# A sliding-window attention and token/channel MLP on one core: fixed buffers and program order on every engine, full 128x128 weight tiles with paired tails, q and k transposed by DMA

## The chip, the cores and the metric

One core of a Trainium2 chip. The metric is the device time of one execution in microseconds (us), as the median of several runs. The kernel before took 393.35 us (three runs, 390.92 to 396.79).

The engines are called by the profile's names: PE (TensorE, matmuls), PEld (its weight loads, which overlap PE), DVE (VectorE), ACT (ScalarE), POOL (GpSimd) and SP (SyncE). POOL issues the loads that cast float32 to bf16, SP the outputs. In the kernels' code PE writes its results into PSUM tiles, which the text also calls banks; those of the new kernel have names that begin with `ps`. `L373` is line 373 of the kernel in question, so line numbers differ from kernel to kernel.

## The reference

Eight batches of 576 tokens, eight heads of 64. Causal attention over a window of 128 keys with a linear bias per head, then an MLP that mixes over tokens and one that mixes over channels.

```
scores = q @ k.T / 8 + slope[h] * -(i - j)         # kept where 0 <= i - j < 128
attn   = softmax(scores) @ v                        # B, H, 576, 64
x      = attn as (B, 576, 512)
h      = relu(x.T @ w_tok1) @ w_tok2                # 576 -> 256 -> 576, over tokens
u      = x + h.T
out    = u + relu(u @ w_ch1) @ w_ch2                # 512 -> 1536 -> 512, over channels
```

576 is four and a half times 128. The half block, 64 tokens, is the tail that this case is largely about.

## The kernel before

A framework schedules it: pools hand out buffers, and the scheduler orders each engine. The MLP of batch b is mixed with the attention of batch b+1. q and k come in token order and are transposed on PE, five blocks per head pair, the last with 64 rows:

```python
for c in range(NCH):                      # 128, 128, 128, 128, 64 tokens
    nc.tensor.transpose(tps[:, s0 : s0 + nn],
                        cbt[tname][:nn, c, hp * 2 * D : (hp + 1) * 2 * D], ident[:nn, :nn])
```

Attention goes by query block and four heads; PV follows the masks of the same four heads at once:

```python
for h in hs:
    nc.scalar.activation(out=pe[:, :, 0:nq], in_=sp[:, i : i + 3 : 2, 0:nq],
                         func=ACT.Exp, bias=biascol[:, h : h + 1], scale=scale)   # one head
    nc.vector.tensor_tensor(out=pb[:, :, 0:nq], in0=pe[:, :, 0:nq], in1=mk[:, :, 0:nq], op=ALU.mult)
# ...
for mi, (o_ap, l_ap, r_ap) in enumerate(mms):        # 65 columns each: 64 of v and a 1
    nc.tensor.matmul(o_ap, lhsT=l_ap, rhs=r_ap, start=(mi == 0), stop=(mi == len(mms) - 1))
```

The second channel matmul makes five passes per batch over the 12 weight blocks, the fifth for 64 tokens only:

```python
for c in range(NCH):
    nq = csz[c]                           # 64 in the last pass
    for ht_i in range(NHT):
        nc.tensor.matmul(o2[:nq, :], lhsT=r2[ht_i][:, c * P : c * P + nq], rhs=WC2[:, ht_i, :], ...)
```

The softmax here doesn't subtract the row's maximum and nothing guards it: scores larger than these inputs give would overflow.

Of the kernel before, what the change touches and what calls it, by code (L numbers as in the profile page):

```python
# [10 lines left out]
ALU = mybir.AluOpType  # L12

DMA_TRANSPOSE_QK = False
DMA_TRANSPOSE_U = False
# [3 lines left out]
def kernel(  # L19
# [11 lines left out]
    nc = tc.nc  # L31
    P = nc.NUM_PARTITIONS

# [5 lines left out]

    assert D == 64 and H % 4 == 0  # L40
    NCH = (S + P - 1) // P
    csz = [min(P, S - c * P) for c in range(NCH)]
    NHP = H // 2
    NQD = H // 4

    slopes = [2.0 ** (-8.0 * (h + 1) / H) for h in range(H)]

    bf16 = mybir.dt.bfloat16
    f32 = mybir.dt.float32

    NDH = DTOK // P
    NCB = DM // P
    NHT = DCH // P
    assert DTOK % P == 0 and DM % P == 0 and DCH % P == 0 and S % 2 == 0
    SH = S // 2

    const = ctx.enter_context(tc.tile_pool(name="const", bufs=1))
    qkpool = ctx.enter_context(tc.tile_pool(name="qk", bufs=2))
    stage = ctx.enter_context(tc.tile_pool(name="stage", bufs=3))
    cbpool = ctx.enter_context(tc.tile_pool(name="cbp", bufs=2))  # L60
    vpool = ctx.enter_context(tc.tile_pool(name="vpl", bufs=2))
    ppool = ctx.enter_context(tc.tile_pool(name="pp", bufs=8))
    xpool = ctx.enter_context(tc.tile_pool(name="xp", bufs=2))
    rpool = ctx.enter_context(tc.tile_pool(name="rp", bufs=2))
    upool = ctx.enter_context(tc.tile_pool(name="up", bufs=2))
    opool = ctx.enter_context(tc.tile_pool(name="op", bufs=3))
    ps_sc = ctx.enter_context(tc.tile_pool(name="ps_sc", bufs=3, space=bass.MemoryType.PSUM))
    ps_ov = ctx.enter_context(tc.tile_pool(name="ps_ov", bufs=2, space=bass.MemoryType.PSUM))
    ps_ma = ctx.enter_context(tc.tile_pool(name="ps_ma", bufs=3, space=bass.MemoryType.PSUM))

    ident = const.tile([P, P], bf16, name="ident")
    make_identity(nc, ident)
    pidx = const.tile([P, 1], f32, name="pidx")
    nc.gpsimd.iota(
        pidx, pattern=[[0, 1]], base=0, channel_multiplier=1,
        allow_small_or_imprecise_dtypes=True,
    )
    biascol = const.tile([P, H], f32, name="biascol")
    for h in range(H):
        nc.gpsimd.tensor_scalar(  # L80
            out=biascol[:, h : h + 1], in0=pidx[:, 0:1],
            scalar1=float(slopes[h]), scalar2=None, op0=ALU.mult,
        )
    patA = const.tile([P, P], bf16, name="patA")
    patB = const.tile([P, P], bf16, name="patB")
    nc.gpsimd.memset(patA[:, :], 1.0)
    nc.gpsimd.affine_select(
        out=patA[:, :], in_=patA[:, :],
        compare_op=ALU.is_gt, fill=0.0, base=0,
        pattern=[[-1, P]], channel_multiplier=1,  # L90
    )
    nc.gpsimd.memset(patB[:, :], 1.0)
    nc.gpsimd.affine_select(
        out=patB[:, :], in_=patB[:, :],
        compare_op=ALU.is_ge, fill=0.0, base=0,
        pattern=[[1, P]], channel_multiplier=-1,
    )

    def _alloc_batch_tiles():
        cbq = cbpool.tile([P, NCH, H * D], bf16, name="cbq", tag="cbq")  # L100
        cbk = cbpool.tile([P, NCH, H * D], bf16, name="cbk", tag="cbk")
        vp = vpool.tile([P, NCH, H, D + 1], bf16, name="vp", tag="vp")
        nc.vector.memset(vp[:, :, :, D : D + 1], 1.0)
        return {"q": cbq, "k": cbk}, vp

    def _dma_qk_chunk(b, cbt, tname, c):
        tens = q if tname == "q" else k
        nn = csz[c]
        s0 = c * P
        nc.gpsimd.dma_start(  # L110
            out=cbt[tname][:nn, c, :].rearrange("p (h d) -> p h d", h=H),
            in_=tens[b, :, s0 : s0 + nn, :].rearrange("h s d -> s h d"),
        )

    def _dma_v_chunk(b, vp, c):
        nn = csz[c]
        s0 = c * P
        nc.gpsimd.dma_start(  # L118
            out=vp[:nn, c, :, 0:D],
            in_=v[b, :, s0 : s0 + nn, :].rearrange("h s d -> s h d"),  # L120
        )

    def attention_dma(b):
        cbt, vp = _alloc_batch_tiles()
        for c in range(NCH):
            _dma_qk_chunk(b, cbt, "q", c)
            _dma_qk_chunk(b, cbt, "k", c)
        for c in range(NCH):
            _dma_v_chunk(b, vp, c)
        return cbt, vp  # L130

    cbt0, vp0 = _alloc_batch_tiles()
    head_chunks = min(2, NCH)
    for c in range(head_chunks):
        _dma_qk_chunk(0, cbt0, "q", c)
        _dma_qk_chunk(0, cbt0, "k", c)
    _dma_v_chunk(0, vp0, 0)
    for c in range(head_chunks, NCH):
        _dma_qk_chunk(0, cbt0, "q", c)
        _dma_qk_chunk(0, cbt0, "k", c)  # L140
    for c in range(1, NCH):
        _dma_v_chunk(0, vp0, c)
    sts_first = (cbt0, vp0)

    qTz = [[const.tile([P, 2, S], bf16, name=f"qTz{hp}_{par}") for hp in range(NHP)]
           for par in range(2)]
    for hp in range(NHP):
        nc.vector.memset(qTz[0][hp][D:P, 0, :], 0.0)
        nc.vector.memset(qTz[0][hp][0:D, 1, :], 0.0)

    masks = const.tile([P, H, 2 * P], bf16, name="masks")
    for h in range(H):
        chA = math.exp(-float(P) * slopes[h])
        nc.vector.tensor_scalar(
            out=masks[:, h, 0:P], in0=patA[:, :],
            scalar1=float(chA), scalar2=None, op0=ALU.mult,
        )
        nc.vector.tensor_copy(out=masks[:, h, P : 2 * P], in_=patB[:, :])

    def attention_steps(b, dma_res, xb):  # L160
        cbt, vp = dma_res
        yield
        qT = []
        kT = []
        for hp in range(NHP):
            for tname in ("q", "k"):
                tps = ps_sc.tile([P, S], bf16, name="tTps", tag="sc")
                for c in range(NCH):
                    nn = csz[c]
                    s0 = c * P  # L170
                    nc.tensor.transpose(  # L171
                        tps[:, s0 : s0 + nn],
                        cbt[tname][:nn, c, hp * 2 * D : (hp + 1) * 2 * D],
                        ident[:nn, :nn],
                    )
                if tname == "k":
                    tt = qkpool.tile([P, S], bf16, name=f"kT{hp}", tag=f"kT{hp}")
                    nc.vector.tensor_copy(out=tt[:, :], in_=tps[:, :])
                    kT.append(tt)
                else:  # L180
                    tt = qTz[b % 2][hp]
                    nc.vector.tensor_copy(out=tt[0:D, 0, :], in_=tps[0:D, :])
                    nc.vector.tensor_copy(out=tt[D:P, 1, :], in_=tps[D:P, :])
                    qT.append(tt)
                yield
        for qb in range(NCH):
            nq = csz[qb]
            q0 = qb * P
            have_a = qb > 0
            nkb = nq  # L190
            for qd in range(NQD):
                hs = [4 * qd + j for j in range(4)]
                hps = [2 * qd, 2 * qd + 1]
                sps = {}
                for hp in hps:
                    sp = ps_sc.tile([P, 4, P], f32, name="sp", tag="sc")
                    sps[hp] = sp
                for half in (0, 1):
                    if half == 0 and not have_a:
                        continue  # L200
                    for hp in hps:
                        spf = sps[hp][:, :, :].rearrange("p b x -> p (b x)")
                        if half == 0:
                            nc.tensor.matmul(  # L204
                                spf[:, 0 : 2 * nq],
                                lhsT=kT[hp][:, q0 - P : q0],
                                rhs=qT[hp][:, :, q0 : q0 + nq],
                                start=True, stop=True,
                            )
                        else:  # L210
                            nc.tensor.matmul(  # L211
                                spf[:nkb, 2 * P : 2 * P + 2 * nq],
                                lhsT=kT[hp][:, q0 : q0 + nkb],
                                rhs=qT[hp][:, :, q0 : q0 + nq],
                                start=True, stop=True,
                            )
# [186 lines left out]
    for b in range(B):  # L403
# [3 lines left out]
        if pending_mlp is not None:  # L407
            gens.append(pending_mlp)
# [56 lines left out]
```

## Time and profile before

| | before |
|---|---|
| median of 3 runs | 393.35 us |
| span of the profiled run | 396.0 us |
| PE busy | 370.6 us (94%) |
| DVE, ACT, POOL busy | 241.0, 195.7, 109.2 us |
| distance between batches | 44.9 us |

Part 1 of the page of the kernel before gives busy time, share of the span and number of instructions of each engine:

```profile
PE 370.6 (94%) x2752; PEld 206.7 (52%) x2752; DVE 241.0 (61%) x792; ACT 195.7 (49%) x593; POOL 109.2 (28%) x147
```

The view by time windows of the kernel before has, per stretch: its length, then busy us and number of instructions of PE, PEld, DVE, ACT and POOL, then the clock granted to PE, the DMA share and GB/s:

```profile
36.00:47.00 11.00, 10.27 (x55) 4.92 (x56) 4.26 (x23) 2.04 (x10) 7.41 (x9) 0.55 0.91 150
60.00:70.00 10.00, 9.93 (x95) 6.74 (x93) 5.34 (x22) 9.61 (x31) 8.06 (x11) 1.00 3.33 126
200.00:210.00 10.00, 9.98 (x94) 5.86 (x93) 7.33 (x29) 8.70 (x27) 3.08 (x4) 1.00 1.20 77
```

After the start PE is hardly ever free, and no other engine is near it. But a busy PE is not a PE at its peak: matmul intervals overlap (190 ns long and 30 ns apart in the new kernel below), so their union hides gaps between starts. The Trainium skill warns of this ("Perfetto Trace Analysis", section "Identifying the Most-Contended Engine": matmul occupancy is no good measure of the distance to the roofline).

The chain of waits of the kernel before (start, duration, what) has the first token-mix matmuls of successive batches, and at its end the last channel matmuls:

```profile
89.61 1.29 PE t_1350 L320 x5
134.50 1.29 PE t_2083 L320 x5
179.40 1.29 PE t_2816 L320 x5
...
359.00 1.29 PE t_5728 L320 x5
...
386.77 2.59 PE o_6001 L388 x12
```

Batches are 44.9 us apart. The last line is the clean rate: twelve matmuls of 512 columns in 2.59 us, 216 ns each.

The timeline of PE in the kernel before (start, duration, line, what, shapes, count) shows how small matmuls stand among large ones:

```profile
138.72 0.20 PE L171 MATMUL tTps<-ident,cbq 64*128 64x64 bf16 x1
138.85 0.34 PE L171 MATMUL tTps<-ident,cbk 128*128 128x128 bf16 x3
...
153.34 0.19 PE L273 MATMUL ot<-vp,pb 128*128 128x65 bf16 x1
153.37 0.27 PE L211 MATMUL sp<-qTz_1_141,kT_2269 128*128 128x256 bf16 x1
153.57 0.20 PE L273 MATMUL ot<-vp,pb 128*128 128x65 bf16 x1
```

Start to start is what counts. After the 64-row transpose at 138.72 the next matmul starts 130 ns later, though it streams half a block. PV matmuls (L273) come one at a time; by the view of waits their weight loads waited 115 times for the mask product, never longer than 0.5 us, 30.3 us in all.

### The profile page before, as it was taken

How to read it: one execution, taken by the hardware profiler on the slowest of the kernel's cores; microseconds unless marked ns; L12 is line 12 of the kernel's file. 1: busy time of each engine (PE TensorE's matmuls, PEld its weight loads, DVE VectorE, ACT ScalarE, POOL GpSimd, SP SyncE). 2: the span in 40 equal slices, each digit the busy share in tenths (PEclk: the TensorE clock that was granted, in tenths of full speed). 3: DMA queues.
4: the chain of work that ended last, by engine and by line, in shares of the span. 5: the costliest groups of instructions: out<-in, count | busy, mean ns of one | idle time of the engine just before them, and what ended most of it. 6: DMA issues, size and time to landing. Idle time of an engine off the chain costs nothing.

```text
span 396.0 us, 7388 instructions
## 1 busy us (share of the span) xinstructions
PE 370.6 (94%) x2752; PEld 206.7 (52%) x2752; DVE 241.0 (61%) x792; ACT 195.7 (49%) x593; POOL 109.2 (28%) x147
## 2 busy tenths in 40 slices
PE   0387999999999999999999999999999999999996
PEld 0143466544754466544764466544764466543752
DVE  7277474766577485766577485776577575765112
ACT  0077229641694238641694328741594327842620
POOL 9996427504440408004350307004000000000000
PEclk9998599999999999999999999999999999999999
DMA  7999999929392379629291379719001200011012
GB/s 48 138 138 100 181 189 129 141 85 73 26 96 79 59 45 86 64 79 74 19 104 53 82 48 81 67 62 91 2 1 55 66 2 0 28 56 40 2 38 82
DMA packets 120804, 27.81 MB, mean 70 GB/s; under 512 B 113280, under 2 KB 115648, under 8 KB 120768
## 3 DMA queue, kind: packets, MB, share of 16 engines
q0 software_dynamic: 115520, 17.90, 72.0%
q1 hardware_dynamic: 5248, 9.44, 6.6%
q8 instruction: 21, 0.34, 0.4%
q14 instruction: 15, 0.12, 0.1%
HBM read 35.78 MB, written 9.44 MB: 114 GB/s over the span
## 4 chain that ended last, share of the span: by engine, by line
PE 87%; POOL 7%; DMA 2%; DVE 2%; ACT 1%; issue 1%; POOLq 0%; ACTq 0%
PE ct L373 23%; PE ot L273 9%; PE tTps L171 6%; PE ht L335 5%; PE sp L211 4%; PE ut L359 3%; PE sp L204 3%; POOL cbq L110 2%; POOL vp L118 2%; POOL cbk L110 2%; DMA W_168<-in_moe_w_tok_dram 2%; DVE ub L341 1%; PE o_5654 L388 1%; PE o_4940 L388 1%; PE o_4207 L388 1%
## 5 line engine op out<-in xcount | busy, mean ns | idle before, releaser
L379 ACT ACTIVATE r2t<-ct 128x288 bf16<-128x288 f32 x192 | 77.4, 454 | 71.6 <-PE ct L373 65.4
L373 PE MATMUL ct<-utt,WC_170 128*128 128x288 bf16 x768 | 110.7, 286 | 0.0
L229 ACT ACTIVATE pe<-sp,biascol 128x256 bf16<-128x256 f32 x192 | 79.1, 587 | 22.7 <-PE sp L211 22.7
L373 PEld LDWEIGHTS <-WC_170 128*128 128x128 bf16 x768 | 69.1, 98 | 16.1
L273 PEld LDWEIGHTS <-pb 128*128 128x128 bf16 (+2 forms) x576 | 41.3, 101 | 67.8 <-DVE pb L233 30.3
L273 PE MATMUL ot<-vp,pb 128*128 128x65 bf16 (+2 forms) x576 | 73.0, 203 | 2.7 <-DVE pb L242 1.2
L118 POOL DMA_DIRECT2D vp<-in_v_dram x40 | 33.8, 870 | 100.0 <-PE o_3532 L388 21.3
L233 DVE TENSOR_TENSOR pb<-pe,masks 128x256 bf16<-128x256 bf16 x192 | 51.8, 287 | 6.4
L388 PEld LDWEIGHTS <-r2t 128*128 128x128 bf16 (+1 forms) x480 | 41.5, 100 | 24.3 <-issue 0.4
L110 POOL DMA_DIRECT2D cbq<-in_q_dram x40 | 35.4, 887 | 52.1 <-PE tTps L171 32.7
L278 DVE RECIPROCAL rt<-ot 128x4 f32<-128x4 f32 (+1 forms) x80 | 14.5, 181 | 41.4 <-PE ot L273 41.1
L341 DVE TENSOR_TENSOR ub<-ht,xb 128x512 bf16<-128x512 f32 (+1 forms) x40 | 24.8, 681 | 22.0 <-PE ht L335 22.0
L110 POOL DMA_DIRECT2D cbk<-in_k_dram x40 | 35.4, 888 | 7.6 <-DMA WC_171<-in_moe_w_ch_dram 6.7
L247 ACT ACTIVATE pe<-sp,biascol 64x64 bf16<-64x64 f32 x64 | 20.0, 313 | 34.0 <-PE sp L211 34.0
L279 DVE TENSOR_TENSOR xb<-ot,rt 128x256 bf16<-128x256 f32 (+1 forms) x80 | 33.9, 423 | 2.0
L171 PE MATMUL tTps<-ident,cbq 128*128 128x128 bf16 (+1 forms) x160 | 20.9, 232 | 11.4 <-DMA cbq<-in_q_dram 11.4
L171 PEld LDWEIGHTS <-cbq 128*128 128x128 bf16 (+1 forms) x160 | 12.6, 101 | 23.8 <-DMA cbq<-in_q_dram 12.2
L171 PE MATMUL tTps<-ident,cbk 128*128 128x128 bf16 (+1 forms) x160 | 20.3, 230 | 4.2 <-DMA cbk<-in_k_dram 3.5
L335 PE MATMUL ht<-r1t,W_169 128*128 128x512 bf16 (+1 forms) x80 | 23.8, 398 | 0.3
L242 DVE TENSOR_TENSOR pb<-pe,masks 128x128 bf16<-128x128 bf16 x64 | 13.2, 223 | 15.9 <-ACT pe L238 14.9
L252 ACT ACTIVATE pe<-sp,biascol 128x64 bf16<-128x64 f32 x64 | 20.0, 313 | 0.0
L171 PEld LDWEIGHTS <-cbk 128*128 128x128 bf16 (+1 forms) x160 | 12.5, 102 | 13.2 <-DMA cbk<-in_k_dram 4.6
(332 smaller groups left out, 454.1 us busy)
## 6 DMA issues: line engine op xcount, KB each, us to landing
out_dram<-obt SPq DMA_DIRECT2D x32, 256.0 KB, 2.0
cbq<-in_q_dram POOLq DMA_DIRECT2D x32, 128.0 KB, 5.1
cbk<-in_k_dram POOLq DMA_DIRECT2D x32, 128.0 KB, 5.3
vp<-in_v_dram POOLq DMA_DIRECT2D x32, 128.0 KB, 5.6
WC_170<-in_moe_w_ch_dram POOLq DMA_DIRECT2D x1, 1536.0 KB, 13.3
WC_171<-in_moe_w_ch_dram POOLq DMA_DIRECT2D x1, 1536.0 KB, 20.2
out_dram<-obt SPq DMA_DIRECT2D x8, 128.0 KB, 3.0
cbq<-in_q_dram POOLq DMA_DIRECT2D x8, 64.0 KB, 5.1
```

Of the source, the lines that this page charges most:

```text
L110: nc.gpsimd.dma_start(out=cbt[tname][:nn, c, :].rearrange("p (h d) -> p h d", h=H), in_=tens[b, :, s0 : s0 + nn, :].rearrange("h s d -> s ...
L118: nc.gpsimd.dma_start(out=vp[:nn, c, :, 0:D], in_=v[b, :, s0 : s0 + nn, :].rearrange("h s d -> s h d"),)
L171: nc.tensor.transpose(tps[:, s0 : s0 + nn], cbt[tname][:nn, c, hp * 2 * D : (hp + 1) * 2 * D], ident[:nn, :nn],)
L229: nc.scalar.activation(out=pe[:, :, 0:nq], in_=sp[:, i : i + 3 : 2, 0:nq], func=ACT.Exp, bias=biascol[:, h : h + 1], scale=scale,)
L233: nc.vector.tensor_tensor(out=pb[:, :, 0:nq], in0=pe[:, :, 0:nq], in1=mk[:, :, 0:nq], op=ALU.mult,)
L273: nc.tensor.matmul(o_ap, lhsT=l_ap, rhs=r_ap, start=(mi == 0), stop=(mi == len(mms) - 1),)
L279: nc.vector.tensor_tensor(out=xb[:nq, qb, hs[0] * D : (hs[-1] + 1) * D].rearrange("p (h d) -> p h d", h=4), in0=ot[:nq, :, 0:D], in1=rt[:n ...
L335: nc.tensor.matmul(ht[:nq, :], lhsT=W2[:, j, c * P : c * P + nq], rhs=r1[j][:, :], start=(j == 0), stop=(j == NDH - 1),)
L341: nc.vector.tensor_tensor(out=ub[:nq, c, :], in0=ht[:nq, :], in1=xb[:nq, c, :], op=ALU.add)
L373: nc.tensor.matmul(ct[:, :], lhsT=WC1[:, cb, ht_i * P : (ht_i + 1) * P], rhs=utb[cb][:, x * SH : (x + 1) * SH], start=(cb == 0), stop=(cb ...
L379: nc.scalar.activation(out=r2t[:, x * SH : (x + 1) * SH], in_=ct[:, :], func=ACT.Relu)
L388: nc.tensor.matmul(o2[:nq, :], lhsT=r2[ht_i][:, c * P : c * P + nq], rhs=WC2[:, ht_i, :], start=(ht_i == 0), stop=(ht_i == NHT - 1),)
```

## The change

The intent: PE is the bound, so take work off it, make every weight tile 128x128, and lay out by hand what comes when. The diff replaces nearly the whole kernel; its core:

```diff
+    ctx.enter_context(tc.manual_schedule())          # program order on all engines
+    psS = [PS(f"psS{i}", [P, 512]) for i in range(2)]; psO = PS("psO", [P, 2, 512])
+    psM = [PS(f"psM{i}", [P, 512]) for i in range(3)]; psT = PS("psT", [P, 512])
 # --- q and k: on PE only for batches 0 and 1
-    nc.tensor.transpose(tps[:, s0 : s0 + nn], cbt[tname][:nn, c, ...], ident[:nn, :nn])
+    def dma_transpose(b):
+        nc.sync.dma_start_transpose(out=kT[i][:, 0:NC]..., in_=kn...)
+        nc.sync.dma_start_transpose(out=kT[i][:, NC, :, 0:ST], in_=knt[:, :])
+        nc.sync.dma_start_transpose(out=qT[i]..., in_=qn...)      # q padded with zeros, 2 x the bytes
+        nc.sync.dma_start_transpose(out=qTt[i]..., in_=qnt...)
 # --- attention by key block: the queries of a key block and of the next one, two heads
+    nc.tensor.matmul(s[:, :], lhsT=kT[i][:, kb, hp, :], rhs=qT[i][:, kb:kb + 2, hp, :, :], ...)
+    nc.scalar.activation(out=e[:, 0:nn], in_=s[:, 0:nn], func=ACT.Exp, scale=scale)   # 512 wide
+    # mask multiply (with the bias in the mask) issued one piece later, PV four pieces later
 # --- tails: two heads side by side in attention, two batches in the second channel matmul
+    nc.tensor.matmul(t[:, :], lhsT=r2t[pi2][:, ht, :, :], rhs=WC2[:, ht, :], ...)     # 2 x 64 tokens
 # --- first channel matmul: 512 columns plus 64
-    rhs=utb[cb][:, x * SH : (x + 1) * SH]                       # 2 x 288
+    rhs=utb[b % 2][:, cb, :]                                     # 512, tail apart
 # --- four of twelve relus on DVE
 # [...] loads, evictions and the order of pieces are cut
+    for it in spread(main, carry):  run(it)     # first channel matmul with 8 pieces of attention b+1
+    for it in spread(seq, fill):    run(it)     # second one and token mix of b+1, with attention b+2
```

## The prediction

> **What bounds the kernel now.** TensorE. In the table of ten-microsecond windows PE is busy 9.9 of every 10 us from 40 to 360 us at clock 1.00. The chain of waits shows the first token-mix matmul (L320) at 89.6, 134.5, 179.4, ... 359.0: 44.9 us per batch, with a head of about 45 us and a tail of 37 us (last MLP alone). I count 88,392 streamed columns per batch. Twelve 512-column matmuls at the end take 2.59 us (216 ns each), so the ideal is 36.8 us; about 8 us per batch are lost around small matmuls. Start-to-start times in the steady timeline: q,k transposes 3.8 us per batch (84 ns per 128x128 one, 135 per 64-row one), 64-row contractions and 64-wide weight tiles 60 to 100 ns dearer, 65-column PV 40 to 110 ns.
>
> **What the change does to PE, per batch.**
> - PE transposes of q,k: removed for batches 2 to 7 (-3.8 us).
> - Tails paired: every weight tile is 128x128; one tail pass of the second channel matmul for two batches (10 passes -> 9). The first becomes 48 of 512 columns plus 48 of 64.
> - Sum from 216 ns per 512 columns and an estimated 37 ns for a tight 64- or 65-column matmul (five of 65 columns end to end in 0.33 us): scores 3.5, PV 2.6, token mix 4.4, u transposes 1.1, channel one 12.3, channel two 11.9 = 36 us. With 1 to 2 us of buffer waits (three rotated PSUM banks) 37 to 38 us per batch.
>
> ACT falls: one 512-column exp per head pair and key block (a 512-column activation took 0.60 us) instead of one of 0.59 per head. DVE takes four relus per batch. I estimate 22 us ACT and 20 us DVE per 37: neither binds.
>
> **What it adds.** Per batch 20 POOL load issues instead of 15, about the same descriptors (0.9 us per 128-partition load), and four DMA transposes on the SP queue, 1.7 MB with the zero padding. The Trainium skill, "DMA: Bandwidth & Descriptors", section "Latency and other measured facts", gives 261 GB/s for a transpose with a non-contiguous middle dimension; that is an estimate of 6.5 us. No run shows it yet; I allow 12. They start behind the previous batch's last output and are needed about 15 us later, so they just hide.
>
> **The start is worse.** POOL issues q,k,v of batches 0 and 1, weights, a clear of qn, then q,k of batch 2. Before's loads ran at 137 GB/s at the start, so I expect q,k of batch 2 to land near 75 us and its transposes near 84, while the second channel matmul of batch 0 with attention of batch 2 mixed in starts near 65. PE then stands 10 to 20 us in program order.
>
> **Time.** Ready with batch 1's token mix at about 100 us; five full iterations of 37 us, one without attention 33 us, last one 27 us: 346 us. Range 328 to 370. Faster by over 2%: 0.94; within 2%: 0.03; slower: 0.03.
>
> **What would show it right or wrong.** Right: batches 37 to 38 us apart; no q,k transpose lines on PE after batch 1; 64-column matmuls at 35 to 40 ns; PE idle at 65 to 85 us released by a DMA transpose. Wrong: score matmuls waiting for DMA transposes in every batch (transposes over 15 us: the period follows them, up to 45 us); 64-column matmuls over 60 ns (+1 to 2 us per batch); POOL solid over the period; scores waiting for exp on two PSUM banks; or no early stall (then about 330).

## The result, and the profile after

The new kernel took 340.28 us (median of 4 runs, 339.55 to 341.18) against 394.18 (4 runs of before on the same chip). The ratio is 0.863, 95% interval 0.856 to 0.869. Ratios here are the mean time of one kernel's fast runs over that of the other's in the same rounds, so they are not quite the ratio of the medians. A second set of runs on another chip gave 339.26 us and 0.864.

Part 1 of the page of the new kernel, span 337.7 us:

```profile
PE 291.4 (86%) x2320; PEld 157.4 (47%) x2360; DVE 168.8 (50%) x397; ACT 158.5 (47%) x319; POOL 129.9 (38%) x170
```

Its chain of waits at the same points:

```profile
66.31 10.50 DMA qT<-qn
...
77.52 1.71 PE psM L338 x4
...
114.07 0.86 PE psM L338 x4
...
151.25 0.86 PE psM L338 x4
...
185.80 0.86 PE psM L338 x4
...
222.98 0.86 PE psM L338 x4
...
257.53 0.86 PE psM L338 x4
...
294.50 0.86 PE psM L338 x4
```

L338 is the first token-mix matmul. From 151.25 to 294.50 are four batches: 35.8 us each, in turn about 37.2 and 34.55, since only odd batches carry a tail pass. The time windows of the new kernel (columns as before):

```profile
60.00:70.00 10.00, 6.02 (x84) 3.81 (x82) 5.43 (x17) 2.21 (x8) 3.81 (x5) 1.00 1.63 112
70.00:80.00 10.00, 3.06 (x8) 1.14 (x9) 0.43 (x1) 0.90 (x2) 2.66 (x4) 0.56 1.22 172
200.00:210.00 10.00, 9.95 (x83) 5.47 (x82) 3.87 (x9) 4.67 (x10) 0.00 (x0) 1.00 0.44 110
```

PE stands for most of 70 to 80 us. The view of waits of the new kernel (who waited for whom: us in all, times, longest) names the cause and the small waits left. A wait of 10.5 us at the very start, for the identity matrix that POOL makes, is left out here; it is in e8 too.

```profile
PE psS L233 <- DMA qT<-qn: 9.5, 1, 9.5
PE psO L303 <- DVE xb L287: 5.0, 8, 1.3
PE psM L372 <- DVE ob L420: 4.2, 7, 0.8
PE psS L233 <- ACT pe L248: 2.1, 6, 0.7
```

Of the six batches with DMA transposes only the first made PE wait. After that wait the granted clock is low (0.56 over 70 to 80 us): the chain has four 512-column matmuls in 1.71 us at 77.52 (428 ns each) against four in 0.86 later.

The timeline of PE in the new kernel shows the small matmuls:

```profile
61.41 0.86 PE L397 MATMUL psT<-utt,WC 128*128 128x64 bf16 x24
...
62.22 0.19 PE L273 MATMUL psO<-vp,pb 128*128 128x65 bf16 x1
62.25 0.19 PE L277 MATMUL psO<-vp,pb 128*128 128x65 bf16 x1
```

They now come in runs with full weight tiles, 30 ns apart. For the 24 of 64 columns: (0.86 - 0.19) / 23 = 29 ns.

### The profile page after: what moved, and what is told of

Its sections match the earlier page's. It is cut to its first block, busy times and chain, and to the rows that moved or that the text cites. A ratio compares the mean times of both kernels' runs of the same rounds, so it can differ in the third digit from the quotient of the medians.

```text
span 337.7 us, 6014 instructions
## 1 busy us (share of the span) xinstructions
PE 291.4 (86%) x2320; PEld 157.4 (47%) x2360; DVE 168.8 (50%) x397; ACT 158.5 (47%) x319; POOL 129.9 (38%) x170
## 4 chain that ended last, share of the span: by engine, by line
PE 76%; DVE 7%; DMA 6%; POOL 6%; ACT 2%; issue 2%; SPq 0%; POOLq 0%; ACTq 0%
PE psM L382 24%; PE psM L415 24%; PE psS L233 5%; PE psM L338 5%; PE psM L349 4%; DMA qT<-qn 3%; PE psM L437 3%; DMA ks<-in_k_dram 3%; PE psM L372 2%; DVE ob L420 2%; DVE r L385 2%; DVE xb L287 2%; PE psT L397 2%; PE psO L277 1%; POOL qs L134 1%
## 5 line engine op out<-in xcount | busy, mean ns | idle before, releaser
L248 ACT ACTIVATE pe<-psS 128x512 bf16<-128x512 f32 (+2 forms) x160 | 80.2, 514 | 65.8 <-PE psS L233 48.7
L382 PE MATMUL psM<-utb,WC 128*128 128x512 bf16 x367 | 88.8, 379 | 2.5 <-ACT utb L374 0.9
L415 PE MATMUL psM<-WC,r 128*128 128x512 bf16 x372 | 89.9, 379 | 0.6
L152 POOL DMA_DIRECT2D qn<-in_q_dram x48 | 36.9, 793 | 95.7 <-DMA qT<-qn 90.2
L257 DVE TENSOR_TENSOR pb<-pe,masks 128x512 bf16<-128x512 bf16 x96 | 38.9, 420 | 36.6 <-ACT pe L248 35.6
L415 PEld LDWEIGHTS <-r 128*128 128x128 bf16 x384 | 36.5, 98 | 39.4
L382 PEld LDWEIGHTS <-WC 128*128 128x128 bf16 x384 | 35.6, 98 | 39.9 <-issue 3.9
L388 ACT ACTIVATE r<-psM 128x512 bf16<-128x512 f32 x64 | 38.2, 597 | 34.1 <-PE psM L382 34.1
L233 PE MATMUL psS<-qT,kT 128*128 128x512 bf16 x96 | 36.6, 389 | 12.5 <-DMA qT<-qn 9.5
L134 POOL DMA_DIRECT2D vp<-in_v_dram x32 | 28.9, 986 | 0.4 <-issue 0.2
L351 DVE TENSOR_TENSOR ub<-psM,xb 128x512 bf16<-128x512 f32 x32 | 21.6, 687 | 10.5 <-PE psM L349 9.8
L134 POOL DMA_DIRECT2D kn<-in_k_dram x24 | 22.6, 943 | 0.0
L338 PE MATMUL psM<-xb,W 128*128 128x512 bf16 x63 | 18.5, 421 | 0.2 <-DMA ks<-in_k_dram 0.2
L277 PEld LDWEIGHTS <-pb 128*128 128x128 bf16 x256 | 15.6, 97 | 5.1 <-issue 1.1
L342 ACT ACTIVATE r<-psM 128x512 bf16<-128x512 f32 x16 | 9.6, 597 | 16.3 <-PE psM L340 16.3
```

What stands on the lines that cost most here:

```text
L134: nc.gpsimd.dma_start(out=dst, in_=src[b, :, c * P:(c + 1) * P, :].rearrange("h s d -> s h d"))
L152: nc.gpsimd.dma_start(out=dst[:, :, 3 * i, :], in_=q[b, i::2, s0:s0 + n, :].rearrange("h s d -> s h d"))
L233: nc.tensor.matmul(s[:, :], lhsT=lhsT, rhs=qT[i][:, kb:kb + 2, hp, :, :], start=True, stop=True)
L248: nc.scalar.activation(out=e[:, 0:nn], in_=s[:, 0:nn], func=ACT.Exp, scale=scale)
L257: nc.vector.tensor_tensor(out=p[:, 0:nn], in0=e[:, 0:nn], in1=mk, op=ALU.mult)
L277: nc.tensor.matmul(ov, lhsT=probs[b, qb, hp][:, i * P:(i + 1) * P], rhs=vt[:, qb, h, :], start=first, stop=(hh == 3))
```

## The experiments

e1, e2, e3, e5, e6 and e8 are edits of the new kernel, e4, e7, e9 and e10 of the kernel before; e11 is e8 in the scheduler's order. Each was timed beside before on its own chip. The diffs show the lines that matter; the rest of each is cut. Before itself falls into two groups of runs: 391 to 394 us with a mean clock of 0.996 to 1.000, and 396 to 399 us at 0.978 to 0.983. For effects of a few us the distance between batches, read in the part at clock 1.00, is therefore the better measure. The record calls the ratios of e4 and e6 to e11 unclear: on their chips only two of before's seven runs are marked fast.

| run | median us | ratio to before | us between batches | PE's largest waits after 40 us |
|---|---|---|---|---|
| before | 391 to 399 | 1 | 44.9 | none over 0.7 us |
| new kernel | 340.28 | 0.863 | 35.8 | 9.5 |
| PE transposes (e1) | 347.9 | 0.880 | 38.65 with transposes | none over 0.8 |
| tails unpaired (e2) | 353.23 | 0.894 | 37.6 | 10.3 |
| late attention 2 (e3) | 332.77 | 0.841 | 35.8 | 2.5 |
| scheduler's order (e5) | 338.96, three of four slow | none | 34.9 | 15.6 |
| before, no transposes (e4) | 375.43 | 0.954 | 41.2 | none over 0.7 |
| before, full tiles (e7) | 377.94 | 0.961 | 42.8 | none over 0.7 |
| before, PV later (e9) | 381.28 | 0.959 | 43.0 | none over 0.7 |
| before, all three (e10) | 353.53 | 0.900 | 38.55 | none over 0.7 |
| exp per head (e6) | 339.35 | 0.865 | 35.8 | 5.3 |
| smoothed (e8) | 322.51 | 0.819 | 34.35 | 2.3 |
| smoothed, scheduler's order (e11) | 336.41 | 0.855 | 34.5 | 7.6 and 11.3 |

### The transposes back on PE (e1)

```diff
-    load_qk_dma(2); dma_transpose(2)
+    load_qk_pe(2)
-        dma_transpose(b + 2)
+        carry = carry + transposes(b + 2)     # within the first channel matmul
```

> The new kernel with q and k of batches 2 to 7 transposed on TensorE as in batches 0 and 1 (done within the first channel matmul of two batches earlier), no DMA transposes. My theory: PE gets 36 more 128-column matmuls per batch at about 57 ns, 2.1 us, for six batches +12.5 us, and the early wait of 9.5 us for the DMA transpose shrinks by about 5: net +5 to +10 us over the new kernel (345 to 350 us). Rival (removing PE transposes is where most of the gain came from, 3.8 us per batch as they cost before): +18 us or more (over 358).

347.9 us, about 8 us over the new kernel and in my range, but its two parts are not as I had them. The chain of waits of this kernel:

```profile
188.14 0.86 PE psM L339 x4
...
228.10 0.86 PE psM L339 x4
...
265.44 0.86 PE psM L339 x4
...
302.40 0.86 PE psM L339 x4
```

The distances are 39.96, 37.34 and 36.96 us. The last has no transposes any more and is as long as in the new kernel (36.97). The other two, with and without a tail pass, stand against 37.18 and 34.55 there. So the transposes cost PE 2.8 us per batch here and not 2.1: 36 of them at 56 ns are 2.0, and PE's small waits, most of them for relus on DVE, are about 0.5 us longer. Six times 2.8 us, less the early wait of 9.5 us, which went altogether and not by 5, is 7.2 us. That the total fell in my range was luck: two misses cancelled.

### The tails of the second channel matmul apart again (e2)

```diff
-    nc.tensor.matmul(t[:, :],    lhsT=r2t[pi2][:, ht, :, :],  rhs=WC2[:, ht, :], ...)
+    nc.tensor.matmul(t[0:ST, :], lhsT=r2t[pi2][:, ht, bi, :], rhs=WC2[:, ht, :], ...)
-        tails = ch2_tail(b) if b % 2 else []
+        tails = ch2_tail(b)
```

> The new kernel with the 64-row tails of the second channel matmul run batch by batch (64-wide weight tiles, 8 passes) instead of two batches in one 128-wide pass (4 passes). My theory: four more passes of twelve 512-column and four 128-column matmuls, 2.85 us each and PE-bound: +11 to +13 us (351 to 354 us). Rival (PE has slack in that stage, or pairing matters only for tile shape): under +4 us.

353.23 us, 13 to 14 us over the new kernel and in my range of totals. Batches are 37.6 us apart, 1.8 more, or 3.5 per pair of batches, which is more than one pass of 2.85: the odd batches, which have a tail pass in both kernels, also take 0.45 us longer (37.63 against 37.18 us) with 64-wide tiles. PE is bound there, and pairing counts in full.

### Attention of batch 2 mixed in late (e3)

```diff
+        lead = 13 if b == 0 else 0
-        for it in spread(seq, fill):
+        for it in seq[:lead] + spread(seq[lead:], fill):
```

> The new kernel with only one thing moved: in the stage of batch 0 with the second channel matmul, attention of batch 2 is mixed in after the 13th of 19 pieces instead of from the start. My theory: the PE wait of 9.5 us for the first DMA transpose disappears, and about 3 us come back as waits for exp where attention is crowded: -5 to -8 us (332 to 336 us). Rival (the wait only moves, because what follows is bound by the loads): within 2 us of the new kernel.

332.77 us: 7 us less than the new kernel, the theory's range. The waits of this kernel that name a DMA transpose shrink to:

```profile
PE psS L233 <- DMA qT<-qn: 2.8, 2, 2.5
```

PE had been standing in program order for data that was on its way, with other work behind it. The wait did not just move.

### The hand order dropped (e5)

```diff
-    ctx.enter_context(tc.manual_schedule())
```

> The same instructions as the new kernel, but the program's hand order dropped: the framework's scheduler orders each engine. If hand order is a main source of the gain: over 350 us. If the instructions are (full weight tiles, paired tails, DMA transposes): within 1% of the new kernel, 337 to 344 us. My guess lies between, 345 to 360 us: single attention matmuls scattered between others wait for their masks as before.

338.96 us, but three of four runs are slow (338.62 to 343.05 at clock 0.963 to 0.970; the fast one 332.72), so there is no ratio, and this run alone decides nothing. My guess of 345 to 360 us was wrong in any case: no run is above 343.05. In the trace, which is of a slow run, PE stood 15.6 us for the first DMA transpose, and in the part at clock 1.00 batches are 34.9 us apart, less than in hand order (35.8). It gave the hint that the order is not what made the kernel fast; e11 below tests that.

### Before without the transposes of q and k (e4)

```diff
+        if b >= 2:
+            qT, kT = list(qTz[b % 2]), list(kTc[b % 2])      # stale
-        for hp in range(NHP):
+        for hp in range(NHP if b < 2 else 0):
```

> The kernel before, with the PE transposes of q and k left out from batch 2 on (stale operands, wrong result on purpose). What these transposes cost where they stand. If they cost what they occupy in the start-to-start times of before, 3.8 us per batch: -20 to -23 us against before. If they cost only their clean stream as in the run with PE transposes in the new kernel, about 2 us per batch: -11 to -14 us.

The chain of waits of this kernel:

```profile
172.98 2.58 PE t L325 x10
214.17 2.58 PE t L325 x10
```

41.2 us apart, 3.7 less than before: where they stood, the transposes cost 3.7 us per batch, not the 2.8 of the new kernel. Runs at like clock (374.6 to 376.4 us against 396.3 to 399.1, all at 0.976 to 0.983; five of these six runs of before are slow) are 22 us apart. The first theory holds. The stale operands passed the comparison with the reference: with inputs of 0.1 times a normal draw I estimate the scaled scores at about 0.01, which the tolerance does not see. So this test of correctness would not catch a wrong transpose either.

### Before padded to full tiles (e7)

```diff
-    csz = [min(P, S - c * P) for c in range(NCH)]
+    dsz = [min(P, S - c * P) for c in range(NCH)]      # for DMAs only
+    csz = [P] * NCH                                     # matmuls over 640 tokens, zeros behind 576
```

> The kernel before with S padded by zeros from 576 to 640 wherever a 64-row or 64-wide tile stood, so that every matmul has a 128x128 weight tile; nothing is paired, and 1,792 more columns per batch stream (0.75 us). My theory (switching between full and partial tiles costs 60 to 100 ns at each partial matmul): about 2.4 us per batch saved, 0.75 given back, -10 to -15 us against before. Rival (those gaps are waits for masks and evictions that happened to be there): no gain or up to 6 us slower.

```profile
168.25 2.16 PE t L337 x10
211.04 2.16 PE t L337 x10
```

That is its chain of waits. Batches are 42.8 us apart, 2.1 less, though 1,792 more columns stream per batch. The ten token-mix matmuls show it in small: 2.16 us here, 2.58 in e4, where two of them contract over 64 rows and stream the same 512 columns. More arithmetic in less time. That the cost lies in the change of tile shape, and not in the half tile itself, shows at the end of PE's timeline in the kernel before:

```profile
386.61 2.75 PE L388 MATMUL o_6001<-WC_171,r2t 128*128 128x512 bf16 x12
389.30 2.78 PE L388 MATMUL o_6017<-WC_171,r2t 128*64 128x512 bf16 x12
```

Twelve half tiles in a row take as long as twelve full ones. Counted from start to start in that trace, 512-column matmuls are 216 ns apart between two tiles of one shape, half or full, and 309 to 319 ns where the shape changes. A batch of before has 43 changes of shape, which take 4.5 us beyond the clean stream; e7 has none. It gives back 0.75 us for the added columns and about 1.5 us in longer waits of transposes and second token-mix matmuls, so 2.1 us are left. Runs at clock 1.00: 377.6 against 391.1 us.

### Before with PV one step later (e9)

```diff
+                if held: held.pop()()      # PV of the four heads before
+                held.append(pv)
-    ppool = ... bufs=8
+    ppool = ... bufs=16
```

> The kernel before with the PV matmuls of four heads issued after the scores, exp and masks of the next four (16 probability buffers instead of 8), so that PV finds its masks ready as in the new kernel. If waits for the mask multiply behind each score are part of the 8 us lost per batch: -4 to -12 us against before. If not: within 2 us.

```profile
166.81 2.58 PE t L327 x10
209.84 2.58 PE t L327 x10
```

43.0 us apart (chain of waits), 1.9 less; at clock 1.00, 377.6 against 391.1 us, a little over my range. The product of exp and mask stood between score and PV of the same heads, and PE paid for it in pieces too small to show as idle time. But the wait is only about half of the 1.9 us: with PV moved, a batch also has 35 changes of tile shape and not 43, worth 0.9 us (from start to start), while the delays before PV matmuls of unchanged shape fell by 0.8 us, from 2.0 to 1.2.

### Before with the three together (e10)

> The kernel before with three parts at once: no PE transposes of q and k from batch 2 on (wrong operands on purpose), full weight tiles by padding, PV one step later. Alone they took 3.7, 2.1 and 1.9 us off the 44.9 us between batches. If these are separate losses, about 0.5 us of overlap (half tiles inside the transposes) apart: 37.5 to 38.2 us between batches, 338 to 346 us in all, and pairing the tails is most of what is left to the new kernel's 35.8. If they are the same idle gaps counted three times: 39.5 us or more, over 355 us.

```profile
160.84 2.17 PE t L349 x10
199.40 2.17 PE t L349 x10
```

38.55 us between batches and 353.53 us: between the two theories. Alone they took 3.7 + 2.1 + 1.9 = 7.7 us, together 6.35, so the overlap is 1.35 us and not 0.5; the total I expected (338 to 346 us) was too low. They are mostly separate losses. What overlaps is the changes of tile shape: e4 has 34 and e9 35 where before has 43, together 1.9 us that full tiles would save again; what makes this more than 1.35 is not shown. From 38.55 to the new kernel's 35.8 are 2.75 us: pairing the tails of the second channel matmul is 1.8 (e2), and the padding columns that the new kernel does not have are 0.75 by count, an estimate (1,792 columns at 216 ns per 512). The rest, about 0.2 us, is the sum of all else that differs, such as the four relus on DVE and the buffer waits; no run takes these apart.

### One exp per head again (e6)

```diff
-            nc.scalar.activation(out=e[:, 0:nn], in_=s[:, 0:nn], func=ACT.Exp, scale=scale)
+            for i2_ in range(2):     # one head each, 256 wide
+                nc.scalar.activation(out=ev, in_=sv, func=ACT.Exp, scale=scale)
```

> The new kernel with the merged exp undone: one exp per head (256 columns) instead of one per head pair (512), in the same program order. My theory (ScalarE has room, 158 of 338 us busy): ACT busy rises by 20 to 30 us in all and the time by less than 3 us over the new kernel. Rival (with two score banks the length of an exp paces the scores): +8 us or more.

Run beside the new kernel itself, as yardstick:

> The new kernel itself on the same chip as the next three, as their yardstick: 340 to 343 us, batches 35.8 us apart in the steady part.

339.35 against 339.26 us (a little under the 340 expected): no difference. Part 1 of its page:

```profile
PE 295.2 (88%) x2320; PEld 158.4 (47%) x2360; DVE 169.5 (50%) x397; ACT 171.7 (51%) x543; POOL 129.8 (38%) x170
```

ACT is busy for 13 us more (158.7 in the yardstick's profile), less than I expected. In the head, where attention of batch 0 runs alone, it costs 2.5 us, but PE then waits 5.3 us instead of 9.9 for the same DMA transpose. Merging the exp is part of the change and gained nothing here; whether the 2.5 us would count without the early wait, no run shows.

### The small waits removed (e8)

```diff
-        lead = ...                          (e3's late attention for batch 2)
+        lead = 13 if b == 0 else 2 if b == 1 else 0
-ATT_IN_CH1 = 8
+ATT_IN_CH1 = 9                      # one more, as the empty piece below counts
-        t = psM[mrot[0] % 3]; mrot[0] += 1
+        t = mfree.popleft()                 # banks in the order in which they come free
+        items.append(lambda: None)          # the tail PV one piece later
         items.append(pv_tail(b))
```

> The new kernel with attention of batch 2 late (piece 13) and of batch 3 a little late (piece 2), PSUM banks of the channel stage handed out in the order in which they come free, and the tail PV one piece later. My theory: 7 to 9 us from the early wait, 3 to 4 us from the waits for the output add (4.2 us in the new profile) and 3 to 4 us from the tail PV behind the normalisation (5.0 us): 322 to 328 us. If those small waits were covered by something else that is late: no better than 331 to 334, as with the late attention alone.

322.51 us, ratio 0.819, interval 0.810 to 0.829. Its waits of PE:

```profile
PE psS L234 <- ACT pe L249: 2.4, 8, 0.6
PE psS L234 <- DMA qT<-qn: 2.3, 1, 2.3
PE psO L304 <- DVE xb L288: 2.1, 2, 1.0
```

The wait for the output add (4.2 us) is down to 0.3 and that for the normalisation went from 5.0 to 2.1. Only the late attention of batch 2 was also run alone (e3); what each of the other edits gave is not shown. The batches are 34.35 us apart, 1.45 less than the new kernel's. This version beats both kernels.

### The same, in the scheduler's order (e11)

> The smoothed kernel with the hand order dropped (scheduler's order). If the order within an engine no longer matters once attention of batch 2 is emitted late and the tiles are full: 318 to 326 us. If the scheduler pulls the scores of batch 2 forward again in front of their transposes: 330 to 340 us with a wait of 5 us or more for a DMA transpose near 65 us.

336.41 us, 14 us more than e8. But its batches, once running, are 34.5 us apart, as in e8. The difference is in two waits near the start:

```profile
PE psM L384 <- DVE ob L422: 11.3, 1, 11.3
...
PE psS L234 <- DMA kT<-kn: 8.5, 2, 7.6
```

The second is the early wait again: the scheduler set the scores of batch 2 in front. The first is new: the output add waited 12.7 us for its buffer, that is for an output DMA, and the chain of waits has the three DMA transposes L172, L175 and L180 on SP from 128 to 135 us in front of it. So the hand order is worth 14 us here, and 0.15 us per batch in the steady part. Going by the starts of the token mix, nearly all of it is the wait for the output add: that of batch 2 starts at 105 us in both kernels, in spite of the early wait, and that of batch 3 at 156.0 against 141.3.

## Why the prediction was right

**The total and its parts.** Predicted 346 us, range 328 to 370; measured 340.28, and 337.7 in the profiled span. The sum by stages:

| stage | predicted | measured in the profile |
|---|---|---|
| until the first channel matmul of batch 1 starts | about 100 | 96.9 |
| five full iterations | 5 x 37 = 185 | 180.7 (36.1 each) |
| the one without attention | 33 | 31.2 |
| the last | 27 | 28.9 |

**The bound.** Right: PE before and after. What counted was the time from start to start, not PE's busy share, which was 94% before and 86% after. The ideal of 36.8 us does not follow from 216 ns per 512 columns, which gives 37.3 for 88,392 columns; the loss in the kernel before is then 7.6 us.

**The distance between batches, 37 to 38 us.** Measured 35.8. The mis-sized term is that of the small matmuls: 37 ns were estimated from five in a row in the trace of before, 29 to 30 ns were measured. The Trainium skill had the better figure: "TensorE: Matmul & The Clock Gate", section "Back-to-back issue gap", gives N / 2.4 + 2.5 ns as the isolated gap of a warm array, which is 29 ns at 64 columns and 216 at 512. This trace agrees with both (29 and 216), though each of these matmuls has its own weight load. With 48 + 12 + 56 such matmuls per batch, 8 ns each are 0.9 us. Of the 1 to 2 us allowed for buffer waits the steady part shows 1.0 (0.6 for the output add, 0.4 for the normalisation). The terms add up to 35.8; less 0.9 and with 1.0 of waits that is 35.9.

**What each part is worth.** The 3.8 us named for the removed transposes is right for the kernel before (3.7 in e4); rebuilt in the new kernel with full tiles they cost 2.8 (e1). A removed piece has two prices, by its surroundings: the nine changes of tile shape that went with the transposes in e4 are as large as the difference. The losses at half tiles (e7) and pairing (e2) were in the prediction, and its 60 to 100 ns are near the 93 to 103 ns measured at a change between 512-column matmuls. The wait of PV for its mask was not named, only its symptom, 65-column matmuls of 40 to 110 ns; of the 1.9 us in e9 about half is that wait.

**ACT and DVE do not bind.** Right: busy 158.5 and 168.8 us, 20 and 21 per batch. e6 shows that ACT's saving gave no time.

**The DMA transposes.** The estimate from the skill ("DMA: Bandwidth & Descriptors", section "Latency and other measured facts", 261 GB/s with a non-contiguous middle dimension) held for the issue of the largest: the 1.05 MB of q kept SP busy for 4.09 us (median), 256 GB/s. Until it landed 6.8 us passed (median), 154 GB/s. All four keep SP for 8.2 us, not 6.5, and take 10 to 12 us from the first issue to the last landing in the steady part, so the 12 allowed were about right. They hide there, as predicted: PE waited for one only once.

**The early wait.** Predicted 10 to 20 us between 65 and 85; measured 9.5 us from 67.4 to 76.9. The loads were done sooner than I said: the q transpose, which waits for them, was issued at 66.3 and not after 75. It then landed late, after 10.5 us, and SP was held 8.4 us by it; loads that ran beside it (172 GB/s in that window) are the likely reason, which no run tests. That the wait came out close is partly luck: the issue was earlier than predicted, the landing slower.

## What to carry to other kernels

When PE is "busy" all the time, measure start to start per shape: half tiles, single small matmuls and waits of a fraction of a microsecond for a mask hide inside overlapping intervals, and here they were 6.35 of 44.9 us per batch (transposes included) before any pairing. Count the changes of tile shape: each cost about 100 ns here. Make every weight tile full, even by padding, and put dependent steps a stage apart. Whether framework or hand ordered the engines mattered little in the steady part (34.5 against 34.35 us per batch). In a hand-ordered kernel look for the one instruction that stands first in line for data that comes late.

## What the Trainium skill lacked or had wrong

- No page has the price of mixing tile shapes; "TensorEngine Tiling (Array Packing)", section "Key Properties", says that a change of tiling mode drains TensorE, but not for how long. Here 512-column matmuls were 309 to 319 ns apart at a change and 216 otherwise, and 43 changes took 4.5 of 44.9 us per batch.
- "TensorE: Matmul & The Clock Gate", section "Back-to-back issue gap", gives about 81 ns per pair of weight load and 128-column matmul as the sustained figure. In the new kernel the 128-column matmuls of the u transposes, each with its own weight load, start 56 ns apart (median of the steady part). Its 131 ns for 512 columns did not appear either: 216 ns is the rate of every clean run here. The formula that the section keeps for an isolated matmul fits both.
- "DMA: Bandwidth & Descriptors", section "Latency and other measured facts", gives bandwidths for the DMA transpose, but no time until the data is usable. Here SP was busy at 256 GB/s, but data was usable at 154 GB/s (1.05 MB landing 6.8 us after issue), and at 100 GB/s (10.5 us) beside loads.
- "ScalarE: Activation LUTs", section "What ACT_TABLE_LOAD costs", gives 280 ns + 0.833 ns per column for a bias by pointer: 493 ns at 256 columns. The exp of before, which reads its 256 columns in two stretches, took 587 ns; e6 reads 256 columns in two stretches too, without a pointer, and its exp took 393 ns, near the page's 399. For the 512-column exp without a pointer it gives 186 + 427 = 613 ns; 601 were measured.
